# Transposes of the first q and k in bf16, a new arrival order, fewer fillers, and two banks for early weighted values, in an attention-plus-MLP kernel

## The chip, the cores and the metric

One core of a Trainium2 chip runs the program. The metric is the device time of one execution in microseconds; lower is better. The engines are TensorE (PE, with weight loads shown apart as PEld), VectorE (DVE), ScalarE (ACT), GpSimd (POOL) and SyncE (SP), which issues most DMA transfers.

## The reference

Attention over q, k, v of shape (4, 8, 768, 64) in f32, where a query sees the 96 positions up to its own and the 8 first (global) ones, with a linear distance bias for each head; then an MLP with softplus on the 3072 tokens.

```python
scores = scale * np.matmul(q, k.transpose(0, 1, 3, 2))
keep = is_global | is_local            # first 8 keys, or 0 <= rel < 96
bias = -slopes[:, None, None] * dist[None, :, :]
scores = np.where(keep, scores + bias[None], -1000000000.0)
a = np.exp(scores - np.max(scores, axis=-1, keepdims=True))
a = a / (np.sum(a, axis=-1, keepdims=True) + 1e-09)
attn = np.matmul(a, v)
x = attn.transpose(0, 2, 1, 3).reshape(B * S, H * D)      # 3072 x 512
h = x @ w_in                                              # 512 x 2048
g = np.maximum(h, 0.0) + np.log1p(np.exp(-np.abs(h)))
out = g @ w_out                                           # 2048 x 512
```

## The kernel before

The 3072 tokens are 24 blocks of 128 (n = 0 to 23). Two neighbouring blocks of one sequence are a unit (i = 0 to 11); their q, k and v are loaded together. Since keys reach back at most 95 positions, a block's scores are taken against its own keys and the block before; the 8 global keys and values are copied into the previous block's key and value tiles (the steps gk, L966, and gv, L976). Two blocks are also a group g of the MLP (0 to 11).

The names of steps, as the code gives them: `ld` and `w` are loads into the ring `raw` of 12 slots of 512 KB; `cast` and `cin`/`cout` cast f32 to bf16 (q and k of early units L841, rows of k and v L865, weights L823); `tr` and `cp` transpose q and k on PE and copy them out of PSUM to `qT` and `kT`/`kTa` (L926, L936, L939; units 0 to 2 only, listed in WIDE); later units transpose by DMA (L953). `sb` seeds PSUM with the bias by a matmul, `sc` are the scores (L1005 for block 0, L1058), `z` adds the bias on DVE (L1084), `ex` is the exponential (L1018, L1091). `pv` multiplies with the values, and a column of ones gives the row sums (L1110); `nm` divides on DVE (L1121, L1122). `xt` and `xc` transpose the result to the MLP's input XT (L1141, L1146; DMA from block 6 on). `a g.p` is the product with w_in for two of the 16 slices of 128 hidden columns (L1168, eight matmuls of 256 columns), `e` and `ln` are softplus as Exp and Ln(1 + .) (L1183, L1194), `b g.ns.x` are pieces of the product with w_out (L1217), `oc` and `st` copy out and store.

Weight pieces: w_in comes in eight pieces of 512 KB (w0 to w7). Slices p = 0, 1 need pieces 0 and 1, p = 2, 3 need pieces 2 and 3, and so on. The eight pieces of w_out are needed in order of the hidden columns.

PSUM has eight banks, and the kernel names them: `s` (two tiles of two banks), `x`, `o`, `h0` and `h1`. A `pv` part (four heads) and its `nm` hold one bank; in the kernel before, PV_KEYS puts both parts of blocks 0, 2 and 3 in `o`.

The order on every engine is fixed when the kernel is built. A planner takes each step's duration, its due time (worked back from the products that need it), and a table of hand-set shifts (NUDGE), and simulates five engines and the DMA queues; at each moment a free engine takes the ready step with the smallest due time. What comes out is one list for each engine, and the chip runs these lists strictly in order. At most eight transfers are outstanding (LANES). Constants of the model are, among others, DMA_FIRST (issue to start of a transfer), FETCH (when an instruction fetch takes DMA time) and each step's price. CHOICE says which engine does a cast or copy. Fillers are matmuls of zeros into bank `x` (L1330) of the lowest rank: PE takes one when nothing else is ready. Each step that uses bank `x` comes after the last filler, since the filler wrote it.

The transposes before are matmuls against the identity, in f32, which write PSUM with a stride:

```python
tr = bank(banks[r]).rearrange("p (x m g a) -> p a x g m", x=2, m=NPAIR, a=4)
for a in range(4):
    c = P * (2 * a + r)
    nc.tensor.matmul(tr[:, a], src[:, c : c + P], ident[:])
```

Of the kernel before, what the change touches and what calls it, by code (L numbers as in the profile page):

```python
# [23 lines left out]
class Planner:  # L24
# [5 lines left out]
    FETCH = 15.5  # L30
    FETCH_COST = 1.0
    DMA_FIRST = 0.75
# [176 lines left out]
FILLERS = 35  # L209
# [5 lines left out]
    0: (("s", 1, 0), ("s", 1, 1), ("s", 0, 0), ("s", 0, 1)),  # L215
    1: (("s", 1, 0), ("s", 1, 1), ("s", 0, 0), ("s", 1, 0)),
    2: (("s", 0, 0), ("s", 1, 0), ("s", 1, 0), ("s", 0, 0)),
# [4 lines left out]
    (0, 1): ("o",),  # L222
    (1, 0): ("o",),
    (1, 1): ("h1",),
    (2, 0): ("o",),
    (2, 1): ("o",),
    (3, 0): ("o",),
    (3, 1): ("o",),
# [37 lines left out]
    "a0.0": -2,  # L266
    "a0.1": -14.5,
    "a0.2": -3,
    "a0.4": 2.25,
    "a1.0": -1,  # L270
    "a1.1": -4.25,
    "a1.2": -3.5,
    "a1.3": -0.5,
    "a1.4": 0.5,
    "a1.6": 15,
    "a1.7": -2,
    "a2.0": 8,
    "a2.2": -11,
    "a2.3": 1.5,
    "a2.4": 4,  # L280
    "a2.5": -10.25,
    "a2.6": -4,
    "a2.7": 8,
    "b0.0.2": 10.5,
    "b0.0.4": -8.5,
    "b0.0.8": -8,
    "b0.1.0": 0.5,
    "b0.1.10": -7.5,
    "b0.1.12": -14.75,
    "b0.1.14": 2.75,  # L290
    "b0.1.2": -1,
    "b0.1.4": 3.75,
    "b0.1.6": -40.75,
    "b0.1.8": 2.75,
    "b1.0.0": 4.75,
    "b1.0.10": 4.5,
    "b1.0.12": -11,
    "b1.0.14": -2,
    "b1.0.2": 1,
    "b1.0.4": -0.5,  # L300
    "b1.0.8": -18.25,
    "b1.1.0": 4.25,
    "b1.1.10": -0.5,
    "b1.1.12": 0.25,
    "b1.1.4": 0.5,
    "b1.1.6": 10,
    "b1.1.8": 55.75,
    "biasFalse0": 2.25,
    "biasFalse2": -2,
    "biasFalse4": 5.5,  # L310
    "biasFalse5": -6.75,
    "biasFalse6": 10,
    "biasFalse7": -5.25,
    "biasTrue0": 1.75,
    "biasTrue2": -2,
    "biasTrue3": 2,
    "biasTrue4": -4,
    "biasTrue6": -0.5,
    "biasTrue7": -1.5,
    "blank": -7,  # L320
    "castk0.0": -2.25,
    "castk0.1": -11.25,
    "castk1.1": 11.5,
    "castk2.0": 4,
    "castk2.1": -8.25,
    "castk3.00": 4.5,
    "castk3.01": -2.5,
    "castk3.10": -0.25,
    "castk3.11": 1,
    "castk4.00": 3.5,  # L330
    "castk4.11": -0.25,
    "castq0.1": 23.25,
    "castq1.1": 16,
    "castq2.0": -17.25,
    "castq2.1": 1.5,
    "castq3.0": 7,
    "castq5.0": 9,
    "castv0.01": 3.5,
    "castv0.10": -1.25,
    "castv0.11": 3,  # L340
    "castv1.00": -13.5,
    "castv1.01": 4,
    "castv1.10": 4,
    "castv1.11": -4.5,
    "castv2.00": 6.5,
    "castv2.01": 8,
    "castv2.10": 8.5,
    "castv2.11": 1.25,
    "castv3.00": 0.75,
    "castv3.10": 0.25,  # L350
    "castv3.11": -20,
    "castv4.00": 1,
    "castv4.10": 0.25,
    "castv4.11": -8,
    "castv6.10": -0.5,
    "castv6.11": -8,
    "cin1": -10,
    "cin2": -3.25,
    "cin3": -67.25,
    "cin4": -0.5,  # L360
    "cin5": -6,
    "cin6": -0.25,
    "cin7": 29,
    "cout0": -6.75,
    "cout1": -19.5,
    "cout3": 0.75,
    "cout4": 2.5,
    "cout6": 6,
    "cout7": -3.25,
    "cpk0.0": -2.75,  # L370
    "cpk1.0": 20.25,
    "cpk1.1": 6.75,
    "cpk2.0": -2,
    "cpk2.1": 9,
    "cpq0.0": 7.25,
    "cpq1.0": -1.25,
    "cpq2.0": 3,
    "d0": -4.25,
    "dl0a": -0.25,
    "dl0b": -0.25,  # L380
    "dl0c": -0.25,
    "dl1a": 0.5,
    "dl1e": 2.5,
    "e0.1": 3.75,
    "e0.2": -4,
    "e0.3": -18.75,
    "e0.4": -1,
    "e0.6": -0.5,
    "e1.0": -2,
    "e1.1": 2,  # L390
    "e1.2": -23,
    "e1.3": 12.5,
    "e1.5": 0.5,
    "e1.6": -1,
    "e1.7": -9.75,
    "e2.3": 2.75,
    "e2.4": -0.5,
    "e2.5": 11.25,
    "ex0.0": 0.75,
    "ex0.1": -8,  # L400
    "ex2.0": -67.75,
    "ex2.1": 2.25,
    "ex3.0": 6.5,
    "ex3.1": -1.5,
    "ex4.0": -23.5,
    "ex4.1": 3.75,
    "ex5.0": -0.25,
    "ex5.1": -26,
    "ex6.0": 0.5,
    "ex6.1": 8.5,  # L410
    "ex7.0": 23.75,
    "ex7.1": 3.75,
    "gk4": 0.5,
    "gk6": 11.75,
    "gk8": 12,
    "gv4.0": -0.75,
    "gv4.1": 1.25,
    "gv5.0": -1,
    "gv5.1": 12,
    "gv6.0": 7,  # L420
    "gv6.1": -6,
    "gv7.1": 0.25,
    "gv8.0": -8,
    "gv8.1": 1,
    "ident": 9.75,
    "iota": -1,
    "ldk0.0": -2,
    "ldk0.1": -6.25,
    "ldk1.0": -5.25,
    "ldk2.0": 0.25,  # L430
    "ldk2.1": 26,
    "ldk3": -4,
    "ldk4": 10.5,
    "ldk5": 1.75,
    "ldq0.0": 1,
    "ldq0.1": 23,
    "ldq1.1": -4,
    "ldq2.0": 12.5,
    "ldq2.1": -4.25,
    "ldq3": -4,  # L440
    "ldv0": 13,
    "ldv3": -8.75,
    "ldv4": -9.5,
    "ldv5": 4,
    "ldv6": -2,
    "ldv7": 16.75,
    "ldv8": 8,
    "ln0.0": 16.5,
    "ln0.2": 4.75,
    "ln0.3": -8.5,  # L450
    "ln1.0": -15,
    "ln1.2": 2,
    "ln2.0": -177.75,
    "ln2.1": 8.75,
    "ln2.2": -8,
    "nm1.0": -12,
    "nm2.0": 7.25,
    "nm2.1": 1,
    "nm3.0": -1,
    "nm3.1": -1,  # L460
    "nm5.0": 2,
    "nm6.0": -12,
    "nm6.1": 1,
    "oc0.0.0": 4,
    "oc0.1.0": 30.25,
    "oc1.0.0": -8,
    "pv0.0": 12,
    "pv0.1": -17.75,
    "pv1.0": -4,
    "pv1.1": 1.25,  # L470
    "pv2.0": 12,
    "pv2.1": -13.75,
    "pv3.0": 0.25,
    "pv3.1": 5.5,
    "pv4.1": 1,
    "pv5.0": -4,
    "pv5.1": 1,
    "pv6.0": 3,
    "pv6.1": -3.25,
    "sb0.0": 2.25,  # L480
    "sb1.1": 17.5,
    "sc0.0": -8,
    "sc1.0": 8,
    "sc1.1": 7.75,
    "sc2.0": 0.5,
    "sc3.0": 9,
    "sc4.0": 7.25,
    "sc5.1": 2,
    "sc6.0": 0.5,
    "sc7.0": -2.25,  # L490
    "st0.0.0": 7.25,
    "st0.1.0": -0.25,
    "st1.0.0": 1,
    "table": -3,
    "trk0.0": 1.5,
    "trk1.0": 1.5,
    "trk1.1": 72.5,
    "trk2.0": -24.5,
    "trk2.1": 1.5,
    "trk4": -2.5,  # L500
    "trq0.0": -36.5,
    "trq1.0": 2,
    "trq2.0": 4,
    "trq2.1": 0.5,
    "trq3": 0.25,
    "trq5": 0.25,
    "win1": -0.5,
    "win5": -16,
    "win6": 1,
    "wout0": -12.5,  # L510
    "wout1": -1.75,
    "wout2": -18.5,
    "wout4": 3.75,
    "wout5": 2,
    "wout7": -11.75,
    "xc1": 5.25,
    "xc2": 1,
    "xc3": 1.75,
    "xc4": 0.25,
    "xc5": -6.5,  # L520
    "xt1": 2,
    "xt2": -82.5,
    "xt4": 5.25,
    "xt5": -2,
    "xt6": -6.75,
    "z2.0": 0.25,
    "z3.0": -8.25,
    "z4.0": -2,
    "z4.1": 15,
    "z5.0": -2,  # L530
    "z6.0": 8,
    "z6.1": -47.25,
    "z7.0": 0.5,
# [21 lines left out]
    "biasFalse0": "POOL",  # L555
    "biasFalse2": "DVE",
    "biasFalse5": "DVE",
# [3 lines left out]
    "biasTrue3": "POOL",  # L561
    "biasTrue7": "DVE",
    "castk0.0": "ACT",
    "castk0.1": "ACT",
    "castk1.0": "POOL",
    "castk1.1": "DVE",
    "castk2.0": "POOL",
    "castk3.00": "ACT",
    "castk3.01": "ACT",
    "castk3.10": "DVE",  # L570
    "castk3.11": "ACT",
    "castk4.00": "DVE",
    "castk4.01": "ACT",
    "castq0.0": "POOL",
    "castq0.1": "ACT",
    "castq1.0": "ACT",
    "castq1.1": "DVE",
    "castq4.0": "POOL",
    "castq5.0": "POOL",
    "castv0.00": "DVE",  # L580
    "castv0.01": "POOL",
    "castv0.10": "ACT",
    "castv1.00": "DVE",
    "castv1.01": "POOL",
    "castv1.10": "DVE",
    "castv2.11": "ACT",
    "castv3.00": "ACT",
    "castv3.01": "DVE",
    "castv3.10": "ACT",
    "castv3.11": "DVE",  # L590
    "castv4.01": "ACT",
    "castv4.10": "ACT",
    "castv4.11": "ACT",
    "cin1": "ACT",
    "cin3": "DVE",
    "cin5": "DVE",
    "cin6": "DVE",
    "cout3": "ACT",
    "cout6": "DVE",
    "cout7": "DVE",  # L600
    "cpk0.0": "DVE",
    "cpk1.1": "ACT",
    "cpk2.1": "DVE",
    "cpq0.0": "ACT",
    "cpq2.1": "ACT",
    "gk4": "ACT",
    "gk5": "ACT",
    "gk6": "ACT",
    "gk7": "ACT",
    "gv4.0": "ACT",  # L610
    "gv4.1": "ACT",
    "gv5.0": "ACT",
    "gv6.0": "DVE",
    "gv8.0": "DVE",
    "oc0.0.0": "ACT",
    "xc1": "ACT",
    "xc4": "ACT",
}
# [12 lines left out]
def kernel(  # L631
# [132 lines left out]
    def load_unit(i, rank, only="qkv"):  # L764
# [4 lines left out]
        for z, which in enumerate(only):  # L769
# [4 lines left out]
            if i in WIDE and which != "v":  # L774
                for y in range(2):

                    on = LOAD_ON.get(f"{which}{i}", "SP")

                    def fn(src=src, raw=raw, y=y, on=on):
                        return dma_on[on].dma_start(  # L780
                            raw[:, 512 * y : 512 * y + 512],
                            src[y::2, sl, :].rearrange("h (g r) d -> g h (r d)", r=8),
                        )

                    op(f"ld{which}{i}.{y}", on, 0.64, rank + 0.01 * z, fn, dma=(0.68, 86.0), sync=sync,
                       writes=[("raw", slot, y)])
                continue
# [92 lines left out]
    def q_of(n):  # L880

        i, x = unit_of(n), n % 2
        t = qT[i % NQT]
        if i in WIDE:
            return lambda rows, m: t[rows, NPAIR * x + m, :]
        v4 = t[:].rearrange("p (r m) t -> p m r t", r=2)
        return lambda rows, m: v4[rows, m, :, 64 * x : 64 * x + 64]
# [612 lines left out]
```

## Time and profile before

| What | Value |
|---|---|
| median of 3 runs | 218.96 us (218.79 to 218.98) |
| profiled execution, time | 219.03 us |
| its span, first to last instruction | 217.2 us |
| ACT busy | 170.7 us, 79% |
| DVE busy | 115.7 us, 53% |
| L1168 MATMUL h_ps, 768 of 128x256 | 95.8 us busy, 273 ns each |
| L1217 MATMUL o_ps, s_ps, x_ps | 384 of 512 columns' worth of work |
| L926 MATMUL s_ps (transposes), 48 | 306 and 311 ns each |
| L1330 MATMUL (fillers), 35 | 11.1 us busy, 442 ns each |
| DMA | 40.95 MB, mean 188 GB/s, near 380 GB/s until about 38 us |

Times are in us, those of single instructions in ns. A row of the timeline has the start, the length, the engine, the line, and in brackets how long the engine had been idle and who released it. A matmul's mean length is longer than its share of PE's time, because matmuls are pipelined: the distance from one start to the next tells what it costs. The profiler's span leaves out 1.83 us at the ends of the execution.

### The profile page before, as it was taken

The numbers are of one execution on the slowest core, as the hardware profiler recorded it, in microseconds if no ns is written. First come the engines' busy times: TensorE is split into PE (matmuls) and PEld (weight loads), VectorE is DVE, ScalarE is ACT, GpSimd is POOL, SyncE is SP. The second block draws the span as 40 slices with busy tenths as digits, with TensorE's granted clock in tenths as the row PEclk, the third lists the DMA queues.
The fourth block names the chain that finished last, engine by engine and source line by source line (L and its number), as shares of the span: only waits on it lengthen the run. The fifth ranks groups of instructions, "written<-read, shape, count | busy, mean of one in ns | idle before, by whom it ended". The sixth has DMA issues, their size and how long they took to land.

```text
span 217.2 us, 4970 instructions
## 1 busy us (share of the span) xinstructions
PE 211.7 (97%) x2003; PEld 144.5 (67%) x2003; DVE 115.7 (53%) x216; ACT 170.7 (79%) x236; POOL 74.4 (34%) x127
## 2 busy tenths in 40 slices
PE   7899999999999999999999999999999999999994
PEld 2576887656665787757767767756766767767554
DVE  6568868674489667327546546446545952101121
ACT  4899999999995699978788688678697878788300
POOL 6316333253059525900265274233236320000000
PEclk9999999999999999999999999999999999999999
DMA  5999999999999399945895996892687212011112
GB/s 202 333 367 387 386 357 367 317 286 214 225 317 175 104 236 264 211 108 155 147 231 160 159 218 165 207 165 72 127 209 198 69 30 75 0 48 53 48 48 97
DMA packets 69846, 40.95 MB, mean 188 GB/s; under 512 B 30144, under 2 KB 61248, under 8 KB 69824
## 3 DMA queue, kind: packets, MB, share of 16 engines
q1 hardware_dynamic: 69392, 40.05, 72.1%
q10 hardware_dynamic: 432, 0.59, 0.9%
q8 instruction: 15, 0.25, 0.5%
q14 instruction: 7, 0.06, 0.1%
HBM read 27.26 MB, written 6.29 MB: 154 GB/s over the span
## 4 chain that ended last, share of the span: by engine, by line
PE 83%; ACT 12%; DMA 2%; issue 2%; SPq 0%; DVE 0%
PE h_ps L1168 34%; PE o_ps L1217 30%; PE s_ps L1058 5%; PE x_ps L1110 4%; ACT pb L1091 3%; ACT e L1183 3%; PE s_ps L1217 3%; PE s_ps L926 2%; DMA raw<-in_k_dram 2%; PE x_ps L1217 2%; ACT g L1194 2%; PE x_ps L1330 1%; ACT vb L976 1%; ACT XT L1146 1%; ACT kb L865 1%
## 5 line engine op out<-in xcount | busy, mean ns | idle before, releaser
L1168 PE MATMUL h_ps<-XT,w_in_bf 128*128 128x256 bf16 x768 | 95.8, 273 | 0.9 <-ACT e L1183 0.7
L1168 PEld LDWEIGHTS <-w_in_bf 128*128 128x128 bf16 x768 | 73.6, 98 | 18.7 <-issue 1.7
L1217 PE MATMUL o_ps<-w_out_bf,g 128*128 128x512 bf16 (+1 forms) x320 | 77.7, 371 | 0.0
L1183 ACT ACTIVATE e<-h_ps 128x512 f32<-128x512 f32 x96 | 59.5, 627 | 20.9 <-PE h_ps L1168 20.5
L1217 PEld LDWEIGHTS <-g 128*128 128x128 bf16 x416 | 37.3, 98 | 28.6
L1084 DVE TENSOR_TENSOR z<-s_ps,biasA 128x1024 f32<-128x1024 f32 x38 | 45.8, 1219 | 15.2 <-PE s_ps L1058 8.6
L1194 ACT ACTIVATE g<-e 128x1024 bf16<-128x1024 f32 x48 | 50.7, 1057 | 1.3
L1091 ACT ACTIVATE pb<-z 128x1024 bf16<-128x1024 f32 (+1 forms) x44 | 43.1, 988 | 7.9 <-DVE z L1084 7.9
L1246 DVE COPY osb<-o_ps 128x512 f32<-128x512 f32 (+1 forms) x20 | 13.4, 670 | 37.1 <-PE o_ps L1217 37.1
L976 POOL COPY vb<-vb 4x512 bf16<-4x512 bf16 x27 | 16.4, 608 | 33.0 <-PE x_ps L1110 28.6
L865 POOL CAST vb<-raw 64x512 bf16<-64x512 f32 x33 | 20.4, 617 | 18.0 <-DMA raw<-in_v_dram 16.8
L865 POOL CAST kb<-raw 64x512 bf16<-64x512 f32 x30 | 18.6, 619 | 19.5 <-DMA raw<-in_k_dram 18.4
L1110 PEld LDWEIGHTS <-pb 128*128 128x128 bf16 x352 | 16.5, 98 | 6.1 <-ACT pb L1091 0.2
L1122 DVE TENSOR_TENSOR xs<-x_ps,rcp 128x256 bf16<-128x256 f32 x40 | 17.0, 424 | 1.4
L1121 DVE RECIPROCAL rcp<-x_ps 128x4 f32<-128x4 f32 x40 | 7.2, 179 | 18.7 <-PE x_ps L1110 18.3
L1110 PE MATMUL x_ps<-vb,pb 128*128 128x65 bf16 x304 | 15.9, 193 | 0.0
L1217 PE MATMUL s_ps<-w_out_bf,g 128*128 128x512 bf16 (+1 forms) x64 | 13.6, 352 | 0.0
L1330 PE MATMUL x_ps<-blank 128*128 128x512 bf16 x35 | 11.1, 442 | 1.2 <-DVE blank L1269 1.2
L1058 PEld LDWEIGHTS <-kT 64*128 64x128 bf16 x224 | 6.8, 94 | 5.1 <-issue 4.9
L1058 PE MATMUL s_ps<-qT,kT 64*128 64x128 bf16 x224 | 9.9, 218 | 0.0
L1084 DVE TENSOR_TENSOR z<-s_ps,bias 128x512 f32<-128x512 f32 x6 | 3.9, 687 | 7.3 <-PE s_ps L1058 7.3
L1246 ACT COPY osb<-x_ps 128x128 f32<-128x128 f32 x1 | 0.3, 266 | 8.7 <-PE x_ps L1217 8.7
(84 smaller groups left out, 120.7 us busy)
## 6 DMA issues: line engine op xcount, KB each, us to landing
raw<-in_v_dram SPq DMA_DIRECT2D x12, 512.0 KB, 5.7
out_dram<-osb SPq DMA_DIRECT2D x23, 256.0 KB, 2.3
raw<-in_q_dram SPq DMA_DIRECT2D x9, 512.0 KB, 4.5
raw<-in_k_dram SPq DMA_DIRECT2D x9, 512.0 KB, 5.6
raw<-in_moe_w_in_dram SPq DMA_DIRECT2D x8, 512.0 KB, 9.5
raw<-in_moe_w_out_dram SPq DMA_DIRECT2D x8, 512.0 KB, 8.6
raw<-in_k_dram SPq DMA_DIRECT2D x6, 256.0 KB, 6.0
raw<-in_q_dram SPq DMA_DIRECT2D x4, 256.0 KB, 8.0
```

The source lines that it names most:

```text
L865: copy_on[eng](dst, src)
L976: copy_on[eng](vb_of(prev)[sl, :, 0:D], vb_of(first)[sl, :, 0:D])
L1058: nc.tensor.matmul(reg if unit_of(n) in WIDE else reg.rearrange("p (r t) -> p r t", r=2), kt[rows, 2 * part + m, :], qv(rows, 2 * part + m ...
L1084: nc.vector.tensor_tensor(z, src, bias, ALU.add)
L1091: nc.scalar.activation(pb[:, 0:nr, :].rearrange("p (y a) b -> p y (a b)", y=2), src, AF.Exp, scale=1.0 / root_d)
L1110: nc.tensor.matmul(xv[:, h, :], pb[:, 4 * (h % 2) + 2 * part + h // 2 if lone else u_all * (2 * (h % 2) + h // 2) + u, :], vb_of(prev if u ...
L1122: nc.vector.tensor_tensor(xs[:, 4 * part : 4 * part + 4, :], xv[:, :, 0:D], rcp[:][:, :, None].to_broadcast([P, 4, D]), ALU.mult,)
L1168: last = nc.tensor.matmul(hv[:, j, :], w_in_bf[:, m, fb * P : fb * P + P], XT[g % NXG][:, m, :], start=(m == 0), stop=(m == NM - 1),)
L1183: nc.scalar.activation(e[:, p % 2, :, :].rearrange("p j (b t r) -> p (j b) r t", b=2, r=2), hb[:].rearrange("p (a r t) -> p a r t", a=4, r=2),
L1194: nc.scalar.activation(gt[:, 2 * p - 2 : 2 * p + 2, :].rearrange("p a t -> p (a t)"), e[:].rearrange("p a j t -> p (a j t)"), AF.Ln, bias=1.0,
L1217: nc.tensor.matmul(bank(key)[:, 0 : z - a], gt[:, fb, ns * P : ns * P + P], w_out_bf[:, fb, a:z], start=(fb == 0), stop=(fb == NFB - 1),)
L1246: copy_on[eng](osb[:, a:z], bank(key)[:, 0 : z - a])
```

## The change

Units 0 to 2: q and k are loaded with partitions in the order head, position instead of position, head; they are transposed as bf16 transposes into contiguous columns of one PSUM bank, and the two copies out of PSUM (one half each) read with a stride. `qT` and `kT` of these units have another order of columns, which scores and gk follow. Both parts of blocks 0 to 3 in `pv` now use two banks, `o` and `x`. There are 18 fillers instead of 35. The planner's constants FETCH and DMA_FIRST and two prices (v0's load, the table) are changed, and with them NUDGE and CHOICE, so the lists of all engines are in another order up to about block 7; from the second piece of `b` of group 2 on PE's list is the same.

```diff
-    FETCH = 15.5
+    FETCH = 18.0
-    DMA_FIRST = 0.75
+    DMA_FIRST = 0.62
...
-FILLERS = 35
+FILLERS = 18
...
 PE_KEYS = {
-    0: (("s", 1, 0), ("s", 1, 1), ("s", 0, 0), ("s", 0, 1)),
-    1: (("s", 1, 0), ("s", 1, 1), ("s", 0, 0), ("s", 1, 0)),
-    2: (("s", 0, 0), ("s", 1, 0), ("s", 1, 0), ("s", 0, 0)),
+    0: (("s", 0, 0), ("s", 1, 0)),
+    1: (("s", 1, 0), ("s", 0, 0)),
+    2: (("s", 0, 0), ("s", 1, 0)),
 }
 PV_KEYS = {
     (0, 0): ("o",),
-    (0, 1): ("o",),
+    (0, 1): ("x",),
     (1, 0): ("o",),
-    (1, 1): ("h1",),
+    (1, 1): ("x",),
     (2, 0): ("o",),
-    (2, 1): ("o",),
+    (2, 1): ("x",),
     (3, 0): ("o",),
-    (3, 1): ("o",),
+    (3, 1): ("x",),
 }
...
-                            src[y::2, sl, :].rearrange("h (g r) d -> g h (r d)", r=8),
+                            src[y::2, sl, :].rearrange("h (g r) d -> h g (r d)", r=8),
...
-            return lambda rows, m: t[rows, NPAIR * x + m, :]
+            return lambda rows, m: t[rows, 2 * m + x, :]
...
-    def transp_pe(i, which, banks, engs, rank):
+    def transp_pe(i, which, key, engs, rank):
...
+        tr = bank(key).bitcast(BF16)
+
+        def mm():
+            for r in range(2):
+                for a in range(4):
+                    c, z = P * (2 * a + r), P * (4 * r + a)
+                    nc.tensor.transpose(tr[:, z : z + P], src[:, c : c + P], ident[:])
...
+        for r in range(2):
+
+            def ev(eng, r=r):
+                copy_on[eng](
+                    dst[:, :, 64 * r : 64 * r + 64].rearrange("p c (g a) -> p c g a", a=4),
+                    tr[:, 512 * r : 512 * r + 512].rearrange("p (a c g) -> p c g a", a=4, g=16),
+                )
...
-        dst = kt_of(prev).rearrange("p m (r t) -> p (m r) t", r=2)[:, :, 0:GH]
+        dst = kt_of(prev).rearrange("p m (r t) -> p m r t", r=2)[:, :, :, 0:GH]
...
-    op("table", "ACT", 1.3, TABLE_RANK, table, writes=["table"])
+    op("table", "ACT", 0.1, TABLE_RANK, table, writes=["table"])
```

In the changed kernel the lines lie two further down in most places: transposes L935, their copies L942, scores L1060, products L1170 and L1219, exponential L1185, fillers L1332. The built lists begin so on PE, in the names above, `fill` for a filler:

```
before: fill x14, trk0 trq0 sb0 fill x5 sc0 fill x2 sb1.0 sc1.0 sb1.1 pv0.0 sc1.1 fill x2 trq1 pv0.1 ...
...     xt0 fill x4 sc2.0 xt1 fill x4 sc3.0 fill sc3.1 pv2.0 fill a0.1 a0.0 pv2.1 a0.3 xt2 a0.2 pv3.0 a0.5
after:  fill x17, trk0 trq0 fill sb0 sc0 sb1.0 sc1.0 sb1.1 sc1.1 pv0.0 pv0.1 trq1 pv1.0 trk1 pv1.1
        xt0 sc2.0 xt1 sc3.0 a0.1 sc3.1 pv2.0 a0.0 pv2.1 a0.3 a0.2 xt2 pv3.1 a0.5 a0.4 pv3.0 a0.7
```

The first loads on SP, in order (ACT issues q0's two pieces): before k0, v0, q1, k1.0, w3, k1.1, v1, w1, w0, w2, w4, w5, w6, w7, q2, k2; after k0, q1, v0, k1.0, w1, k1.1, w0, w3, v1, w4, w2, w5, w7, w6, k2, q2.

## The prediction

> **What bounds the kernel now.** I read first the page's busy times and the chain of work that ended last.
>
> ```profile
> PE 211.7 (97%) x2003; PEld 144.5 (67%) x2003; DVE 115.7 (53%) x216; ACT 170.7 (79%) x236; POOL 74.4 (34%) x127
> ...
> PE 83%; ACT 12%; DMA 2%; issue 2%; SPq 0%; DVE 0%
> ```
>
> TensorE (PE) is both the busiest engine and 83% of the chain; ScalarE's (ACT's) 12% lie between 16 and 50 us. The end thus moves by what PE saves where it has no gaps, and by how much earlier its gapless stretch begins. So I read the opening in the timeline.
>
> ```profile
> 6.79 1.05 PE L926 MATMUL s_ps<-ident,kb 128*128 128x128 bf16 x8 [0.62 <-ACT kb L841]
> ...
> 8.98 1.24 PE L1330 MATMUL x_ps<-blank 128*128 128x512 bf16 x5
> ...
> 16.24 1.03 PE L1330 MATMUL x_ps<-blank 128*128 128x512 bf16 x4
> ...
> 18.55 0.57 ACT L1146 COPY XT<-o_ps 128x512 bf16<-128x512 bf16 x1
> ...
> 20.06 1.91 PE L1168 MATMUL h_ps<-XT,w_in_bf 128*128 128x256 bf16 x16
> ...
> 22.45 1.03 PE L1168 MATMUL h_ps<-XT,w_in_bf 128*128 128x256 bf16 x8 [0.36 <-ACT e L1183]
> ...
> 23.32 0.39 PE L1141 MATMUL o_ps<-ident,xs 128*128 128x128 bf16 x4
> ...
> 23.55 1.04 PE L1168 MATMUL h_ps<-XT,w_in_bf 128*128 128x256 bf16 x8
> ```
>
> The first work is at 6.79, after the first keys have landed (0.72 + 0.66 issue, DMA to 6.09 in the chain) and been cast. Up to the first product of the MLP (L1168) at 20.06, 21 of the 35 fillers (L1330) plug PE's holes: PE waits there for the attention's steps on ACT and VectorE (DVE). From 22.45 on it is nearly full. Last I read the transfers, one issue per narrow window, with its start from the DMA queue's timeline.
>
> ```profile
> 9.95 1.66 SPq L821 DMA_DIRECT2D raw<-in_moe_w_in_dram  x1
> ...
> raw<-in_moe_w_in_dram SPq DMA_DIRECT2D x1, 512.0 KB, 10.5
> ...
> 20.06:50.00 29.94, 29.13 (x288) 21.68 (x287) 23.07 (x43) 29.19 (x45) 12.78 (x16) 1.00 1.11 337
> ```
>
> An issue at 9.95 lands at 20.45: eight transfers are always outstanding and land in order. Issue plus latency gives each landing, and the distance of landings the price of one: 0.68 us for a 256 KB piece of q or k, 1.36 for 512 KB of weights, 1.75 for 512 KB of v, with one hole of 0.95 between 18.15 and 20.45. The last line shows PE, ACT and DMA (share 1.11) all full from 20 to 50 us; ACT is busy 29.19 of 29.94.
>
> **The change, part by part.** The sum is made against the profiled execution, 219.03 us: 217.2 of span and 1.83 around it. The median, 218.96, is 0.07 less.
>
> *Transposes.* The chain has eight of L926 in 0.87 us, 109 ns each. The four contiguous bf16 ones of L1141 begin at 23.32 and the next instruction at 23.55: 57 ns each. All 48 save 48 x 0.052 = 2.5 us of PE; 32 of them lie in the opening, among holes, and count only through it. The 16 of unit 2 lie in the full stretch: 0.83.
>
> *Their evictions.* No row has this form (bf16 read from PSUM at a stride of 128 elements). Nearest on DVE: 0.416 for contiguous bf16 (L1146) and 0.691 for f32 (L936); on ACT 0.56 and 0.58. I take the f32 rows, the other being contiguous. The Trainium skill, VectorE: DVE Perf Modes, Mode 2×_1P, says two 16-bit values go per cycle only at a step of one. L1146 against L936 agrees for the contiguous case; by the rule the price is 0.69, by the other row the sum would be about 0.1 better, since ACT bounds what follows.
>
> *Opening.* The built program's order gives who stands behind whom. Seventeen fillers come first: nine cold at 0.43 (weight loads 0.43 apart until 4.93), eight at 0.216, to 6.8, when the first keys are cast as now; so they cost nothing, and if they ended later, all would shift by as much. Sixteen transposes end at 7.7. ACT's two half evictions end at 8.6; DVE casts q1.0 first, which lands at 6.09 + 2 x 0.68 = 7.45, then evicts two halves of 0.69, to 9.3. The first scores can start at 9.4, now 10.16. But ACT casts three pieces of v before its first exponential, and v now lands behind q1, at 7.45 + 1.75 = 9.2: 9.2 + 3 x 0.52 (starts of such casts lie 0.52 apart) = 10.8, now 10.95. Almost all of the early evictions' gain is lost there.
> Behind it ACT starts, by the distance of starts in its timeline: four exponentials 2.9 (to 13.7), weight piece 0 0.96, two half evictions 0.96, first copy to XT 0.47, copy and cast of v 1.06, second XT copy 0.5: 17.6. The first a0 can start at 17.7 instead of 20.06. Weighted values in two banks (part 1 in x) take part 1 out of the queue behind part 0's normalization: PV of block 0 runs as a pair at about 12 us, now 12.23 and 14.05; that gain is inside this chain, and its cover is ACT.
>
> *Next wait.* The third a0 needs weight pieces 2 and 3. The new arrival order by the prices above: v0 9.2, k1.0 9.9, w1 11.25, k1.1 11.95, w0 13.3, w3 14.65, v1 16.4, w4 17.8, the hole, w2 20.1. Its cast on POOL takes 1.1 (L823 mean 1.119): 21.3, against 22.45 now. PE has by then the same list behind it: gain 1.1. ACT's list comes to this point at 22.3, now 23.74. The gap of some 1.5 us before it is where 2.36 at the first a0 become 1.1.
>
> *From there to 50.* Unit 2's transposes give 0.83. The holes before 27.49 and 49.47 (0.5 and 0.26) mostly go, as ACT's list is shorter: priced by shape, about 2.2 us less up to the 20th exponential e. I count 0.6. Were PE to run without any hole, its list up to a2.1 is 26.7 us, to 48.0, with four more pieces of w_out's product (4 x 0.432) done than now at 49.47: gain 3.2. Lower end: the 1.1 alone. I take 1.1 + 0.83 + 0.6 = 2.5.
>
> *After 50.* From the second piece of b2 (about 68 us) the built order is the same on PE; only shifts remain. Next late would be block 6's scores (55.64 now): its DMA transposes land at 45.25 + 5.9 = 51.2 and 48.67 + 3.4 = 52.0, a slack of 3.6 that covers 2.5.
>
> *The rest at nothing.* Loads with partitions in h-g order: still 128 rows of 2 KB. If they ran like v (0.875 per 256 KB), the eight pieces would bring w2 1.6 later; if like weights, 0.68, nothing changes, which I take. The planner's constants, the table's price and the ranks change only the order, counted above. The gk copies, now with one dimension more for units 0 to 2: 0.2 each (L966), as now.
>
> Sum: 219.03 - 2.5 = 216.53; less 0.07: 216.5.
>
> **Rivals.**
> *The clock drops.* PE has from 8 to 17.7 us only about 4.9 us of work, no fillers, holes up to 1.1. The trace shows half speed only at the start (0.43 against 0.216, for 3.8 us), no such sparse stretch: price zero, or half speed until 3.8 us of dense work. Then transposes and PV take about 1.0 longer on the way to XT, the first a0s take 1.74 instead of 0.87, and the third starts at about 23.2: 1.9 of 2.5 are gone, 218.4. Against: no hole near 3.8 us.
> The Trainium skill, TensorE: Matmul & The Clock Gate, Part 4 and A second HAM failure mode, says that transposes do not count as PE work for the clock and that frequent short idling can make it oscillate; this speaks against the change, and the trace, full of fillers, can't decide it.
> *Evictions slow.* If the strided reads cost double, 1.15 on ACT and 1.38 on DVE, ACT has five halves more, +2.9 by e0.6, and DVE's pair delays the first scores by 1.4. ACT's list comes to its fourth ln 1.1 earlier by my count; with 2.9, less 0.7 of idle ahead of v, it is 1.1 late, and 0.83 of PE's saving is left unused behind it: 219.03 + 0.9 = 219.9, slower. It decides above about 0.95 us on ACT. For: no row. Against: every row of 512 elements, whatever the layout, is 0.56 to 0.63 there.
> *The transfers hide it.* DMA is full to 50 us and the bytes are the same, so if block 6 to 8's inputs become PE's wait, only 0 to 0.5 is left: 218.7. Against: 3.6 of slack.
>
> **How the numbers follow.** Forecast 0.57, own range 215.7 to 217.9; clock 0.13; transfers 0.12; slow evictions or a similarly longer ACT list 0.18. Under 218.5 (0.2%, what this measurement can tell): all of the forecast, most of clock (0.11), half of transfers (0.06): 0.74. Within: 0.08. Slower: 0.18. The range, 215.7 to 218.9, leaves out the slower case and a little below.
>
> **What would show it.** First a0 at about 17.7, the third at 21.3 released by POOL's w_in cast; L935 in 57 ns steps; L942 at 0.58 and 0.69; a2.1 near 47.5. The clock: 128x512 rows more than 0.25 apart after 8 us, or a0's eight in 1.7. Wrong: e later than now at its 8th, DVE evictions near 1.3, or idle on PE before L1060 past 50 us.

## The result and the profile after

The changed kernel took 247.0 us (median of 5 runs, 246.68 to 247.44) against 218.96 (218.79 to 219.36, 5 runs): 1.128 times as long, 95% interval 1.126 to 1.130. The forecast was 216.5, with 218.9 as the upper end. The profiled execution took 246.68 us, 244.9 of it span.

These lines of the page after answer to those of the page before; `PEclk` and `DMA` are the granted clock and the DMA engines' share in tenths, 40 slices of 6.1 us.

```profile
span 244.9 us, 4906 instructions
...
PE 212.2 (87%) x1959; PEld 144.6 (59%) x1986; DVE 113.0 (46%) x212; ACT 169.7 (69%) x232; POOL 81.4 (33%) x138
...
PE   8144479437999999999999999999999999999995
...
PEclk9957757956999999999999999999999999999999
DMA  1348794796989899699738947959759721410022
...
PE 66%; DMA 15%; SPq 9%; ACT 6%; issue 1%; DVE 1%; POOL 1%; DVEq 0%; ACTq 0%; POOLq 0%
```

PE is as busy as before (212.2 us against 211.7), ACT too (169.7 against 170.7). Nothing was added to any engine; the 27.7 us more of span are waiting, all in the first ten slices. In the chain, DMA and SP's queue, 2% together before, hold 24%. The chain in order of time names the waits (start, length, what):

```profile
3.00 4.09 SPq L786
7.13 3.46 SPq L796
10.65 5.88 SPq L786
...
21.38 13.44 DMA raw<-in_v_dram
...
36.27 1.05 POOL w_in_bf L829
...
38.15 18.08 DMA raw<-in_q_dram
```

L786 is the load of a piece of q or k, the line whose order of dimensions the change turned round. Three issues in a row hold SP for 4.09, 3.46 and 5.88 us; with the old order of the load the same three take 0.59 to 0.60 (first experiment below). The limit of eight outstanding transfers does not explain this, since the last of the three is only the eighth transfer; why an issue takes longer while slow pieces are under way was not looked into. The chain then goes over v of unit 1, which lands at 34.82, GpSimd's casts of it and of a piece of w_in, and the issue of a piece of q of unit 2 at 37.32, which lands at 56.23. PE itself waits for the casts of q and k, as its timeline shows:

```profile
15.82 1.01 PE L935 MATMUL s_ps<-ident,kb 128*128 128x128 bf16 x8 [8.89 <-ACT kb L847]
...
31.14 1.03 PE L935 MATMUL s_ps<-ident,kb 128*128 128x128 bf16 x8 [3.28 <-POOL kb L847]
...
36.05 1.87 PE L1170 MATMUL h_ps<-XT,w_in_bf 128*128 128x256 bf16 x8 [0.39 <-ACT XT L1148]
...
48.78 0.62 PE L935 MATMUL s_ps<-ident,kb 128*128 128x128 bf16 x8 [3.08 <-POOL kb L847]
...
56.89 1.01 PE L935 MATMUL s_ps<-ident,qb 128*128 128x128 bf16 x8 [5.96 <-DVE qb L847]
```

The first transposes come at 15.82 (before 6.79), the first product with w_in at 36.05 (20.06), 16.0 us late. The holes before unit 2's transposes bring the delay to 27.6 at the ninth product, and the span ends 27.7 later. Why the loads are late, the windows say (stretch, length, busy time and count of PE, PEld, DVE, ACT, POOL, then granted clock, DMA share, GB/s). After:

```profile
2.00:6.00 4.00, 4.00 (x13) 1.56 (x12) 2.41 (x11) 1.17 (x1) 0.96 (x3) 1.00 0.25 73
6.00:10.00 4.00, 0.93 (x5) 0.20 (x3) 0.00 (x0) 1.63 (x6) 0.00 (x0) 1.00 0.26 102
14.00:18.00 4.00, 2.18 (x18) 1.93 (x19) 0.00 (x0) 2.30 (x6) 0.60 (x2) 0.50 0.26 96
```

Before:

```profile
2.00:6.00 4.00, 4.00 (x13) 1.42 (x11) 3.19 (x13) 1.81 (x4) 2.73 (x6) 1.00 0.95 317
6.00:10.00 4.00, 3.38 (x26) 2.53 (x25) 2.12 (x5) 3.86 (x10) 0.84 (x3) 1.00 1.06 343
14.00:18.00 4.00, 4.00 (x55) 2.88 (x53) 3.27 (x11) 3.65 (x6) 1.71 (x2) 1.00 1.07 392
```

Where q or k are loaded, the DMA engines' mean share is a steady quarter, and some 100 GB/s move instead of 320 to 390. A quarter of 16 engines is four. In the pattern `h g (r d)` the slowest dimension is the four heads; in `g h (r d)` it was the 32 groups of positions. So the theory (A): a transfer is spread over as many engines as its slowest dimension gives, four here, and a piece of 256 KB costs 256 KB / 96 GB/s = 2.7 us instead of 0.68. The packets in the traces bear this out: from 3 to 6 us, 16 are in flight at the median before and four after (those of 4 bytes left out), while one of 2 KB takes 84 ns in both; four times 2 KB in 84 ns are 98 GB/s. The Trainium skill, DMA: Bandwidth & Descriptors, Why a DMA increments its semaphore by 16 and not by 1, has this rule: the number of engines is the largest up to 16 that divides the slowest dimension longer than one of both patterns; the share of 0.25 agrees. The same windows show a second thing, a granted clock of 0.50 in 14 to 18 us, where PE starves.

### The profile page after: what moved, and what is told of

The parts are those of the page before. It is cut to its first block, busy times and chain, and to the rows that moved or that the text cites. A ratio compares the mean times of both kernels' runs of the same rounds, so it can differ in the third digit from the quotient of the medians.

```text
span 244.9 us, 4906 instructions
## 1 busy us (share of the span) xinstructions
PE 212.2 (87%) x1959; PEld 144.6 (59%) x1986; DVE 113.0 (46%) x212; ACT 169.7 (69%) x232; POOL 81.4 (33%) x138
## 4 chain that ended last, share of the span: by engine, by line
PE 66%; DMA 15%; SPq 9%; ACT 6%; issue 1%; DVE 1%; POOL 1%; DVEq 0%; ACTq 0%; POOLq 0%
PE h_ps L1170 28%; PE o_ps L1219 25%; DMA raw<-in_q_dram 7%; SPq L786 6%; DMA raw<-in_v_dram 5%; PE x_ps L1112 4%; PE s_ps L1219 4%; PE s_ps L1060 3%; ACT e L1185 2%; DMA XT<-xs 2%; PE x_ps L1219 2%; ACT pb L1093 2%; SPq L796 1%; SPq L827 1%; ACT g L1196 1%
## 5 line engine op out<-in xcount | busy, mean ns | idle before, releaser
L1170 PE MATMUL h_ps<-XT,w_in_bf 128*128 128x256 bf16 x768 | 98.0, 277 | 0.8 <-ACT XT L1148 0.4
L1170 PEld LDWEIGHTS <-w_in_bf 128*128 128x128 bf16 x768 | 74.4, 99 | 19.3 <-issue 0.8
L1219 PE MATMUL o_ps<-w_out_bf,g 128*128 128x512 bf16 (+1 forms) x295 | 74.4, 371 | 1.4 <-issue 0.2
L1185 ACT ACTIVATE e<-h_ps 128x512 f32<-128x512 f32 x96 | 59.8, 628 | 22.3 <-PE h_ps L1170 21.7
L1219 PEld LDWEIGHTS <-g 128*128 128x128 bf16 x416 | 37.3, 98 | 28.8
L871 POOL CAST vb<-raw 64x512 bf16<-64x512 f32 x36 | 22.4, 621 | 15.7 <-DMA raw<-in_v_dram 14.4
L871 POOL CAST kb<-raw 64x512 bf16<-64x512 f32 x30 | 18.3, 611 | 19.7 <-DMA raw<-in_k_dram 18.6
L1124 DVE TENSOR_TENSOR xs<-x_ps,rcp 128x256 bf16<-128x256 f32 x44 | 18.7, 425 | 1.5
L1112 PE MATMUL x_ps<-vb,pb 128*128 128x65 bf16 x328 | 17.5, 195 | 0.1
L847 DVE CAST qb<-raw 128x1024 bf16<-128x1024 f32 (+1 forms) x8 | 5.0, 622 | 26.3 <-DMA raw<-in_q_dram 26.2
L935 PE MATMUL s_ps<-ident,kb 128*128 128x128 bf16 x24 | 2.7, 279 | 15.2 <-ACT kb L847 8.9
L1219 PE MATMUL s_ps<-w_out_bf,g 128*128 128x512 bf16 (+1 forms) x62 | 13.1, 352 | 0.1
L935 PEld LDWEIGHTS <-kb 128*128 128x128 bf16 x24 | 2.0, 125 | 16.0 <-issue 9.4
L847 POOL CAST qb<-raw 128x512 bf16<-128x512 f32 (+1 forms) x5 | 3.9, 784 | 20.4 <-DMA raw<-in_q_dram 12.1
L1060 PE MATMUL s_ps<-qT,kT 64*128 64x128 bf16 x224 | 9.9, 218 | 0.0
```

Source lines behind the costliest of these rows:

```text
L871: copy_on[eng](dst, src)
L1060: nc.tensor.matmul(reg if unit_of(n) in WIDE else reg.rearrange("p (r t) -> p r t", r=2), kt[rows, 2 * part + m, :], qv(rows, 2 * part + m ...
L1112: nc.tensor.matmul(xv[:, h, :], pb[:, 4 * (h % 2) + 2 * part + h // 2 if lone else u_all * (2 * (h % 2) + h // 2) + u, :], vb_of(prev if u ...
L1124: nc.vector.tensor_tensor(xs[:, 4 * part : 4 * part + 4, :], xv[:, :, 0:D], rcp[:][:, :, None].to_broadcast([P, 4, D]), ALU.mult,)
L1170: last = nc.tensor.matmul(hv[:, j, :], w_in_bf[:, m, fb * P : fb * P + P], XT[g % NXG][:, m, :], start=(m == 0), stop=(m == NM - 1),)
L1185: nc.scalar.activation(e[:, p % 2, :, :].rearrange("p j (b t r) -> p (j b) r t", b=2, r=2), hb[:].rearrange("p (a r t) -> p a r t", a=4, r=2),
```

## Experiments

**The order of the load alone, both ways.** First the changed kernel with the old order of the load; the heads and positions of units 0 to 2 are then mixed.

```diff
-    src[y::2, sl, :].rearrange("h (g r) d -> h g (r d)", r=8),
+    src[y::2, sl, :].rearrange("h (g r) d -> g h (r d)", r=8),
```

> The changed kernel with one line put back: q and k of units 0 to 2 are loaded with partitions in position-head order as before; all else stays, so heads and positions of these units are mixed up in the output, while every instruction keeps its shape. Theory A (the head-position loads are confined to 4 of 16 DMA engines, a quarter of the rate: DMA share 0.25 while only they are in flight): the opening is back, DMA share near 1.0 between 2 and 10 us, and the time is 216 to 219 us, my forecast of 216.5 without the load term. Rival B (fewer fillers and the clock, slow strided evictions, or the new lists are what costs): it stays above 235 us, with the granted clock below 1 in the first 60 us.

Measured: 219.34 (218.80 to 221.38, 10 runs) against 219.0; ratio 1.0025 (0.9996 to 1.0054). The whole loss is gone, but so is the hoped-for gain. Then the kernel before with the new order of the load and nothing else:

```diff
-    src[y::2, sl, :].rearrange("h (g r) d -> g h (r d)", r=8),
+    src[y::2, sl, :].rearrange("h (g r) d -> h g (r d)", r=8),
```

> The kernel before with only the loads of q and k of units 0 to 2 in head-position order; heads and positions are mixed up in the output, all else is as before. Theory A: each of the 12 pieces takes 4 x 0.68 = 2.7 us instead of 0.68, 24.5 us more in all, so 240 to 246 us, DMA share 0.25 in the first 6 us. Rival B: within 2 us of 219.

Measured: 245.57 (244.74 to 245.98); ratio 1.120 (1.117 to 1.123), 26.6 us more than before. Twelve pieces (units 0 to 2, q and k, two each) at three times 0.68 more are 24.5. The one line costs almost what the whole change costs.

**Eight instead of four.** The piece is cut as eight heads by 16 groups of positions instead of four by 32, so the slowest dimension is eight; same bytes, same 2 KB runs.

```diff
-    src[y::2, sl, :].rearrange("h (g r) d -> h g (r d)", r=8),
+    src[:, P * (b0 + y) : P * (b0 + y) + P, :].rearrange("h (g r) d -> h g (r d)", r=8),
```

> The changed kernel with the same pieces cut the other way: eight heads times 16 rows of positions instead of four heads times 32, so the slowest dimension of the load is 8, with runs of 32 KB in DRAM instead of 64 KB; heads and positions are mixed up in the output. Theory A by its count: 8 of 16 engines, DMA share 0.5 in the first 6 us, a piece at 1.36 us, 12 x 0.68 = 8 us over the first experiment: 224 to 230 us. Rival C (the long contiguous runs in DRAM are slow in themselves, whatever the engines): share and time stay near the changed kernel's, 0.25 to 0.3 and above 238 us.

Measured: 232.88 (232.64 to 233.81); ratio 1.064 (1.061 to 1.066): between the theories' figures, nearer A. Its window decides for A's mechanism:

```profile
2.00:6.00 4.00, 4.00 (x12) 1.49 (x11) 2.81 (x11) 2.18 (x5) 0.89 (x3) 1.00 0.49 155
```

The share is 0.49 at 155 GB/s, twice that of the changed kernel (0.25, 73). The edit also halves the contiguous stretches in DRAM (32 KB instead of 64), so a rival by which longer stretches are read more slowly could give the same ratio. Against it stand the packets: from 3 to 6 us eight are in flight at the median, and one of 2 KB still takes 84 ns, as before and after. The price of the time was too low: doubling twelve pieces gives 8.2 us over the 219.34 of the first experiment, measured are 13.5. Some of the rest is the clock (0.50 in 14 to 18 us here too); how much was not separated.

**The rest of the change, computing the reference.** Old load order, and the eviction sorts the columns into the same places with one dimension more:

```diff
-    dst[:, :, ...].rearrange("p c (g a) -> p c g a", a=4),
-    tr[:, ...].rearrange("p (a c g) -> p c g a", a=4, g=16),
+    dst[:, :, ...].rearrange("p (m x) (g a) -> p m x g a", x=2, a=4),
+    tr[:, ...].rearrange("p (a x g m) -> p m x g a", a=4, x=2, g=16),
```

> Position-head loads as in the first experiment, and the copies out of PSUM read one dimension more (head, half, position, element), so that the whole reference is computed: the rest of the change without its load order. Theory A: as the first experiment within 1 us, 216 to 219.5 us, with DVE evictions at 0.69 us and ACT's at 0.58. If the strided reads cost double (my rival of slow evictions), 219.5 to 221 and L942 rows near 1.2 us.

Measured: 220.08 (218.71 to 221.26, 12 runs); ratio 1.0043 (1.0020 to 1.0067): slower than before by 0.9 us. The evictions' group rows, VectorE's and ScalarE's, with busy time and mean ns:

```profile
L942 DVE COPY qT<-s_ps 128x512 bf16<-128x512 bf16 x4 | 2.7, 689 | 1.1 <-ACT qT L942 0.9 <-PE s_ps L935 0.2
...
L942 ACT COPY qT<-s_ps 128x512 bf16<-128x512 bf16 x2 | 1.2, 586 | 0.0
```

The time lies in the range of the rival with slow evictions, but the rows do not: they cost the same as the f32 rows they replace, so they are not what is missing. The windows of this kernel, and PE's timeline where the MLP begins, show what is:

```profile
16.00:20.00 4.00, 1.80 (x24) 1.33 (x25) 3.09 (x6) 3.93 (x9) 3.26 (x5) 0.92 1.06 376
20.00:24.00 4.00, 4.00 (x37) 2.81 (x36) 2.06 (x5) 3.26 (x6) 3.29 (x5) 0.65 1.05 386
```

```profile
17.08 0.40 PE L1060 MATMUL s_ps<-qT,kTa 64*128 64x128 bf16 x8 [1.26 <-ACT kTa L942]
...
19.33 1.87 PE L1170 MATMUL h_ps<-XT,w_in_bf 128*128 128x256 bf16 x8 [0.70 <-ACT XT L1148]
```

PE works 1.80 us of the four from 16 on, and the granted clock falls: 0.65 in 20 to 24 us. The first product's eight matmuls take 1.80 us from 19.33 to the next instruction's start instead of the 0.87 of before (16 from 20.06 to 21.80). From 16 to 20 us the kernel before, with its 35 fillers, had PE busy 4.00 of 4.00, at full speed. The twelve runs go with the clock on record: the three with a mean of 1.000 took 218.71 to 219.33 us, two with 0.990 218.92 and 219.71, three with 0.992 220.03 to 220.22, and four with 0.984 220.17 to 221.26. So theory D: the clock rival of the prediction is real, and was only hidden behind the loads.

**Matmuls of zeros in the holes.** To the kernel above, 18 are put after planning into PE's holes between 8 and 19 us; no list changes otherwise.

```diff
+    plug = {"sb0.0": 4, "pv0.1": 2, "pv1.0": 2, "xt0": 5, "xt1": 2, "sc3.0": 3}
     for o in order:
         o.ins = o.fn()
+        for j in range(plug.get(o.name, 0)):
+            nc.tensor.matmul((x_ps if o.name == "sb0.0" else h_ps[1])[:], blank[:, 0:P], blank[:])
```

> The kernel of the experiment with position-head loads and the whole reference computed, its lists unchanged, and 18 zero matmuls put into PE's holes between 8 and 19 us (4 in bank x before the first scores, 14 in bank h1 between block 0's exponential and the first a0). Theory D (with the loads mended, what is left over is the clock: PE idles so much before 19 us that it is granted half speed until about 25 us): granted clock 1.00 throughout, the first a0's eight matmuls in 0.87 us instead of 1.8, median 217.3 to 218.3 and runs within 1 us of each other, against 220.08 with runs from 218.7 to 221.3. Rival E (the longer way through v, ACT and the weights is all): 219 or more, with the fillers only taking PE's time.

Measured: 218.21 (217.97 to 218.81, 12 runs) against 218.88; ratio 0.9973 (0.9956 to 0.9990), and the runs lie within 0.84 us instead of 2.55. By the ratios the zeros bring 0.7%, 1.5 us. In the profile the clock reads 1.00, and the rows agree, eight matmuls of a product taking 0.87 us (20.70 to 21.57):

```profile
16.00:20.00 4.00, 3.97 (x36) 2.10 (x36) 3.28 (x6) 3.75 (x8) 3.64 (x5) 1.00 1.06 375
20.00:24.00 4.00, 3.71 (x44) 2.95 (x43) 2.25 (x5) 3.98 (x7) 3.06 (x5) 1.00 1.05 387
```

```profile
20.70 1.03 PE L1170 MATMUL h_ps<-XT,w_in_bf 128*128 128x256 bf16 x8
21.57 0.29 PE L1112 MATMUL x_ps<-vb,pb 128*128 128x65 bf16 x4
```

The rows are needed here, since this execution has no record of the clock, and a view then shows 1.00; a second profile of this kernel (below) has one, at full speed from 5.61 us to the end. The clock may not account for the whole gain: the three runs above that kept it were no faster than the kernel before (median 219.06 against 219.0). By these few runs some 0.7 of the 1.5 us has another cause, which stays open.

**Fewer fillers in the kernel before.** Its lists unchanged, the last 17 of its 35 fillers left out.

```diff
     for o in order:
+        if o.name in [f"fill{j}" for j in range(18, FILLERS)]:
+            continue
         o.ins = o.fn()
```

> The kernel before with its lists unchanged, but without the last 17 of its 35 fillers (those from 9.6 us on). Theory D: the granted clock falls to half before 20 us, the first a0s run at half speed, and the time is 0.8 to 3 us above 219, with a wider spread. Rival E: within 0.3 us of 219.

Measured: 219.33 (218.44 to 220.06); ratio 1.0015 (0.9994 to 1.0035). D's 0.8 or more did not come. The window:

```profile
16.00:20.00 4.00, 1.80 (x35) 1.19 (x33) 3.92 (x8) 3.95 (x8) 2.08 (x2) 1.00 1.05 386
```

PE is as thin here, 1.80 of 4.00, and in this execution the clock stays whole. In 12 to 16 PE is busier (3.35 against 2.69). But six of the twelve runs show a mean clock of 0.991 or 0.992, while no run of the kernel before on that chip is below 0.998: without these fillers the clock does drop, in half of the runs, at less cost than D forecast.

The clock records of the traces show what may decide. The clock changes only at steps of 3.41 us, which lie differently in each run: half speed from 19.35 to 22.77 with the loads mended, from 18.49 to 25.32 (two steps) in the first experiment. In the step just before, PE was busy 34% and 50%; here the two steps from 13.95 on have 71% and 62%. All eleven drops ahead of a run's end, in the traces that have such records, follow a step with PE busy 50% or less, and no step with 53% or more is followed by one. Two steps (44% and 46%, in the kernel with eight heads) have no drop behind them, and no run was made to test this, so it is a pattern and not a rule.

**The head of the program.** In the plugged kernel's profile the first transposes stood behind fillers until 7.79 (7.07 in the kernel without the zeros), which looked like a cost of TensorE warming up late. Four of the 17 head fillers are skipped; the plugged kernel runs beside it.

```diff
     for o in order:
+        if o.name in ("fill13", "fill14", "fill15", "fill16"):
+            continue
         o.ins = o.fn()
```

> The plugged kernel (loads position-head, whole reference computed, 18 matmuls of zeros in PE's later holes) without four of the 17 fillers at its head. In the plugged kernel's profile the head fillers ended at 7.79, a microsecond after the keys were cast, and the first transposes waited for them. Theory D (the late end of the cold fillers is on the opening's path when TensorE warms up late, and fewer of them still leave it warm from 8 us on): 217.3 to 218.0, with the first transposes at 6.8 to 7.0. Rival E (the head's end is hidden behind the third piece of v and ScalarE's exponentials, as the forecast had it for the early evictions): 218.0 to 218.4, no difference from the plugged kernel. Rival F (with fewer fillers TensorE is still at half speed at the transposes, or falls back to it later): above 218.6.

> The plugged kernel as before, on the same chip as the one with 13 head fillers, to be compared with it: 217.9 to 218.6 by its earlier runs, and faster than the kernel before by 0.1 to 0.4%. If it comes out above 218.8, its earlier gain was the chip's and not the kernel's.

Measured: 218.63 (ratio 0.9971, 0.9955 to 0.9988) and 218.66 (0.9976, 0.9961 to 0.9990), against 219.11: no difference, which is the mark of rival E; both lie just above the ranges forecast for them, on a chip where the kernel before is slower too. Theory D of the head falls. In the profile of the kernel with 13 the transposes come no earlier:

```profile
7.73 0.61 PE L935 MATMUL s_ps<-ident,kb 128*128 128x128 bf16 x8 [1.61 <-POOL bias L1310]
```

PE sat idle 1.61 us before them, so in this execution it was not the fillers that held them: the second piece of k landed late, and ACT cast it from 6.97 to 7.59 (6.05 to 6.67 in the first profile of the plugged kernel). The second run also confirms the small gain of the first.

**Where the remaining gain goes.** With the loads mended and the zeros in, the change brings 0.5 to 0.7 us, not 2.5. Comparing the starts of the products with w_in, the plugged kernel leads the one before by 0.79 us at the first, and by 0.33 at the ninth. From 30 to 50 us the windows of the kernel before, in one line:

```profile
30.00:50.00 20.00, 19.90 (x190) 13.45 (x188) 15.20 (x25) 19.36 (x31) 8.40 (x10) 1.00 1.14 315
```

and of the plugged one:

```profile
30.00:50.00 20.00, 19.32 (x176) 12.34 (x177) 14.35 (x25) 19.68 (x29) 8.89 (x10) 1.00 1.12 318
```

PE's idle time has grown from 0.10 to 0.68 while ACT is busy 19.68 of 20. Theory G: ACT, not PE, now bounds this stretch. Its list holds six copies of global values of 4x512 between 6 and 50 us (three in the kernel before), 0.61 us each, while GpSimd is busy 8.89 us of the 20 from 30 on. The test puts five of them on GpSimd, and in a second kernel all six; the order of everything else stays.

```diff
     for o in order:
-        o.ins = o.fn()
+        o.ins = o.inner("POOL") if o.name in ("gv5.1", "gv6.0", "gv6.1", "gv8.0", "gv8.1") else o.fn()
```

> The plugged kernel with five of ScalarE's copies of global values (4x512, 0.61 each, at 32.32, 39.64, 42.81 and two from 48.35 in its profile) put on GpSimd instead, nothing else moved; TensorE's, VectorE's and the loads' lists are the same. Theory G (from 22 to 50 us ScalarE's full list bounds the MLP's first groups, 9.86 of 10 us busy, so that the lead of 0.8 at the first product with w_in has become 0.3 at the ninth): TensorE's holes between 30 and 50 (0.35 and 0.33 in the plugged kernel) close, and the end comes 0.4 to 0.8 earlier: 217.4 to 218.2. Rival H (TensorE's own list, or transfers, bound that stretch): within 0.2 of the plugged kernel, 218.0 to 218.8. Rival I (GpSimd's casts of w_out behind the copies become late): above 218.8.

> As the kernel with five copies of global values on GpSimd, and a sixth one too: ScalarE's copy at 17.48, between its two copies to XT, ahead of the second of them, which the first product with w_in waits for. Theory G, with ScalarE as the bound of the opening too: the first product with w_in comes at 18.6 to 18.9 instead of 19.0 to 19.4, and the time is another 0.1 to 0.6 below that of the kernel with five. Rival (GpSimd casts the first values of unit 1 and w_in's pieces 0.6 later, and the third product waits for them): 0 to 0.6 above the kernel with five.

Measured against 219.32 on that chip: five copies 217.67 (ratio 0.9931, 0.9905 to 0.9956), six copies 217.40 (0.9915, 0.9889 to 0.9941). The kernel with five:

```profile
30.00:50.00 20.00, 19.98 (x184) 12.83 (x183) 16.14 (x27) 18.01 (x26) 12.52 (x16) 1.00 1.09 317
```

ACT has fallen to 18.01 and PE's idle time to 0.02. G holds; by the ratios the five copies are worth 0.4%, 0.9 us, slightly above the forecast. The plugged kernel and this one were measured on different chips, each against the kernel before, and their intervals meet at 0.9956; that PE's holes closed is what shows the cause. The 0.27 us between five and six copies lie within the intervals. The sixth did not bring the first product forward as expected (19.17, not 18.6 to 18.9): ACT's copy to XT ended at 18.46, but three of the zeros, from 18.51 on, now stood ahead of the product.

**Without those three zeros.**

```diff
-    plug = {"sb0.0": 4, "pv0.1": 2, "pv1.0": 2, "xt0": 5, "xt1": 2, "sc3.0": 3}
+    plug = {"sb0.0": 4, "pv0.1": 2, "pv1.0": 2, "xt0": 5, "xt1": 2}
```

> The kernel with six copies on GpSimd, without the three matmuls of zeros directly ahead of the first product with w_in (18.51 to 19.17 in its profile, where ScalarE had finished the second copy to XT at 18.46). Theory: the zeros now stand in the way; the first product starts at 18.6 to 18.8 instead of 19.17, and if ScalarE's list leaves room the time is up to 0.4 below the kernel with six, 216.9 to 217.4. Rival one: ScalarE's four exponentials from 18.35 on decide the third product anyway, and the time stays within 0.1 of the kernel with six. Rival two: the granted clock falls to half near 20 us again, as in the kernel without zeros: 0.8 to 1.8 above.

> The kernel with six copies on GpSimd and all 18 zeros, on the same chip as the one with 15: 217.0 to 217.9, ratio to the kernel before 0.989 to 0.994, as in its first runs. Above 0.996 would mean that the first result was the chip's.

Measured: 217.21 (216.80 to 217.68; ratio 0.9921, 0.9901 to 0.9942), and the one with all 18 zeros 217.73 (0.9932, 0.9910 to 0.9955), against 219.07. PE's timeline of the kernel with 15:

```profile
18.36 1.05 PE L1170 MATMUL h_ps<-XT,w_in_bf 128*128 128x256 bf16 x8
...
21.62 1.92 PE L1170 MATMUL h_ps<-XT,w_in_bf 128*128 128x256 bf16 x16 [0.66 <-ACT pb L1093]
```

The first product now starts at 18.36, 0.65 earlier than in the run beside it (19.01), but only 0.4 is left at the third (21.62 against 22.00). The row names ACT's exponentials as what it waited for; GpSimd's cast of a piece of w_in ended at 21.57 as well, and that is what the third product waits for in the run beside it, so which of the two decides is not shown. The medians differ by 0.5 us and the intervals overlap: a gain of this edit is likely but not shown. Both beat the kernel before, by 0.7 to 0.8%.

## Why the prediction was wrong

**The step that failed** stands under "The rest at nothing": "Loads with partitions in h-g order: still 128 rows of 2 KB. If they ran like v (0.875 per 256 KB), the eight pieces would bring w2 1.6 later; if like weights, 0.68, nothing changes, which I take." The runs showed 2.7 us for a piece, three times the worse bound. Bytes and row lengths were compared with rows of v and of weights, and from those rows a bound was made. But no load of the kernel before had so short a slowest dimension (32 groups of positions was the shortest), so no row could show what that does; the bound held only for transfers over all engines. The line was also the only one in the diff that touched a transfer's pattern, on a resource that the windows had shown full (1.11 from 20 to 50 us). The range was thus wrong by the same step: its only case of slower loads was the 1.6 us later w2. "The transfers hide it" had them only at the old price.

**Transposes** were right: eight of L935 follow their predecessors by 0.44 us in the kernel with mended loads (starts 7.07 and 7.51), 55 ns each against the 57 forecast.

**Evictions** were right: 0.68 to 0.69 us on DVE and 0.58 to 0.59 on ACT in the changed kernel itself, against 0.691 and 0.58. The rival of slow evictions is refuted.

**The clock** was priced at zero, with a rival at 0.13 that gave 218.4. With the loads mended the rival happened: half speed near 20 us, first product 1.80 us for eight. The argument against it, "no hole near 3.8 us", asked for one long hole; a stretch with PE busy 2.69 and then 1.80 of 4 us, no hole above 1.5, was enough there. The kernel before without its 17 fillers kept the clock in half of its runs, so the rival's "half speed until 3.8 us of dense work" was not certain either. In the changed kernel as it is, the stretches of half speed up to 60 us follow the starved PE.

**The opening** was too hopeful. The first product was put at 17.7 and comes at 19.3 to 19.5 with the old load order, 0.5 to 0.7 before the kernel before rather than 2.4. The chain of landings slipped: v0 at 9.63 (forecast 9.2), k1.0 at 11.48 (9.9), w0 at 15.17 (13.3) in the first experiment; why they slipped stays open. The three casts of v took 1.89 rather than the 1.56 counted.

**"The holes ... mostly go, as ACT's list is shorter"** was wrong in place. Summing ACT's instructions in the traces of the plugged kernel and of the one before, its list is 2.5 us shorter at the 20th e (54.7 against 57.2; forecast 2.2), but 1.5 longer at the 12th (36.0 against 34.5). The saving comes after the stretch that needed it, and unit 2's 0.83 went into PE's holes from 30 to 50. That ACT was the wait which takes PE's place there was shown by moving the five copies.

**After 50**, "only shifts remain" was right: from the product at 73 us on, the differences between the kernels change by 0.4 at most in the plugged and the mended kernel, and by 0.3 in the changed one.

## What to carry to other kernels

A load's cost is not given by its bytes and its row length: read its slowest dimension, and compare it with those of the rows from which the price is taken; a DMA share at a plain fraction such as a quarter, with few GB/s and SP stuck on issues, is its mark. A price bounded "by the nearest rows" is only a bound if those rows vary in what the edit changes. And where a change thins PE's work, look at the granted clock, in more than one run, and where it shortens PE's list, at the next engine's list up to the same point, not over the whole stage.

## What was not expected of the hardware

With four packets of 2 KB in flight instead of 16, at the same 84 ns each, the loads moved 73 GB/s from 2 to 6 us and 96 to 102 later; eight gave 155 from 2 to 6. The DMA engines' shares were 0.25 to 0.26 and 0.49: the order of two dimensions in a pattern, with the same bytes in the same runs of 2 KB, cost 26.6 us of 219. The granted clock went to half with PE busy 1.80 us of four in one kernel and stayed whole with the same 1.80 in a run of another, whose runs lost it in six of twelve cases; it changed only at steps of 3.41 us. And 18 matmuls of zeros, 3.9 us of work by the 0.216 of one, paid for themselves.
